# Where the cluster logits stand in PSUM, and where their comparison with the maximum is kept

## The chip, the cores and the metric

The program runs on one core of one Trainium2 chip. The metric is the device time of one execution in microseconds (us). Of the kernel before, three timed executions took 779.81, 781.78 and 782.66 us; their median, 781.78 us, is the time before. One further execution was recorded by the hardware profiler: it took 783.62 us, and the span from its first to its last recorded instruction is 781.8 us.

## The reference

Clustered attention is followed by a token-mixing layer. Every query and every key is given to one of 16 clusters, the one whose centroid it points at most; a query sees only the keys of its own cluster.

```python
q_assign = np.argmax(np.einsum('bhsd,hcd->bhsc', q_n, c_n), axis=-1)
k_assign = np.argmax(np.einsum('bhsd,hcd->bhsc', k_n, c_n), axis=-1)
mask = q_assign[:, :, :, None] == k_assign[:, :, None, :]
scores = scale * np.matmul(q, k.transpose(0, 1, 3, 2))
scores = np.where(mask, scores, -1000000000.0)
attn = softmax(scores)                  # written out there: minus the max, exp, over the sum + 1e-9
x = np.matmul(attn, v)                  # 4 batches x 8 heads x 768 tokens x 64
theta = x @ w_theta                     # x as 4 x 768 x 512 from here on
y = einsum(w_tok_r, x * cos(theta)) + einsum(w_tok_i, x * sin(theta))
u = x + y
out = u + np.maximum(u @ w_ch, 0.0)
```

The change touches only the `argmax`. It is computed as the first of the largest: the 16 logits of a token are compared with their maximum, the equal ones are weighed with the falling numbers 16, 15, ..., 1 (`wb`), and the largest weight names the cluster.

## The kernel before, in words

**Attention.** Two heads that lie in partitions 0 to 63 and 64 to 127 form a pair; there are 16 pairs (`pi`). A pair has 12 units `u`: two halves `a` of 384 queries, times six tiles `i` of 128 keys. For each unit and each head `j` of it TensorE computes a score tile `sc` of 128 keys x 384 queries in four matmuls (`score_products`: three products of high and low parts, and one that adds the mask and the row maximum), ScalarE takes the exponential out of PSUM (`exps`, L487), GpSimd adds the exponentials up (L498), and TensorE weighs the values with them (`weighted`, L559). Ten units ahead of the scores, TensorE computes the same products the other way round into tiles `m` (`max_products`), whose row maximum VectorE takes (`max_of`, L433).

**The order around the change is written out by hand.** The loop takes two units at a time, and each engine keeps the order in which the code issues. For the even unit `u` TensorE gets: the scores of `u` for both heads, interleaved (`both`); the scores of `u + 1` for head 0, interleaved with an `m` tile; the values of units `u - 2` and `u - 1` (eight `av` matmuls); then the pieces that are due at `u`; then the scores of `u + 1` for head 1, interleaved with another `m` tile. `score_products` and `max_products` are issued through `interleave` (L411). Preparatory work for later pairs is cut in pieces, due at units that stand in tables (`A_UNITS` for the clusters). `assign(pi)` loads a pair, computes its 16 x 2 logits per token (`lg`, copied to `lgs`), turns them so that tokens stand in the partitions (`turn_logits`, three 128 x 128 transposes into a tile `lt`, L300), takes the maximum and compares (`find_max`, L305 and L307), and in its next piece weighs and reduces (`first_of`, L312 and L314). The turn is due two units before the first scores of pair `pi - 1`, right after the eight `av` matmuls. Pairs 0 and 1 go through the same functions before the loop begins, so 14 pairs go through them in it.

**PSUM** has 8 banks. Pool `ps0` holds two tiles of two banks each for `m`; pool `ps` holds three single banks, which the score tiles use in turn, together with `lg`, `ot`, `mt` and `sm`; pool `ps_av` has one bank for `av`. A tile gets a bank when the earlier tile in it has been read for the last time: its first writer waits for that reader. An engine works off its own instructions strictly in order, so what stands behind a waiting matmul waits too.

**Then** the token-mixing layer follows: rotation angles (`tp`), mixing over tokens (`y`), and the channel layer (`cp`, `cy`). The change does not touch it.

Of the kernel before, what the change touches and what calls it, by code (L numbers as in the profile page):

```python
# [14 lines left out]
ALU = mybir.AluOpType  # L15
# [28 lines left out]
def kernel(  # L44
# [19 lines left out]
    nc = tc.nc  # L64
    B, H, D, S = qT.shape
    P = 128
    NP = H // 2
    NT = S // P
    C = cent.shape[0] // H
    DM = w_theta.shape[0]  # L70
    NCT = DM // P
    HS = S // 2
# [130 lines left out]
    def m_tile(name):  # L203
        return ps0.tile([P, 2, 512], F32, tag="m", name=name)

    def bank(name):
        return ps.tile([P, 512], F32, tag="bank", name=name)
# [58 lines left out]
    NG = HS // C  # L266

    wb = wc.unsqueeze(1).broadcast_to([P, NG, C])
# [23 lines left out]
        return lgs  # L292

    def turn_logits(pi, lgs):
        lt = (m_tile(f"lt{pi}")[:, 0] if pi > 1 else bank(f"lt{pi}"))[:, 0:HS]
        ltp = lt.rearrange("p (g a t c) -> p a g t c", a=2, t=NH, c=C)
        for t in range(HS // P):
            sl = slice(t * P, (t + 1) * P)

            nc.tensor.transpose(out=ltp[:, :, :, t], in_=lgs[:, sl], identity=identf)  # L300
        return lt.rearrange("p (g c) -> p g c", c=C)

    def find_max(pi, ltv):
        mx = pe.tile([P, NG], F32, tag="mxl", name=f"mxl{pi}")
        nc.vector.tensor_reduce(out=mx, in_=ltv, op=ALU.max, axis=AX.X)  # L305
        eq = pe.tile([P, NG, C], BF16, tag="eq", name=f"eq{pi}")
        nc.vector.tensor_tensor(  # L307
            out=eq, in0=ltv, in1=mx.unsqueeze(2).broadcast_to([P, NG, C]), op=ALU.is_equal)
        return eq

    def first_of(pi, eq):
        nc.vector.tensor_tensor(out=eq, in0=eq, in1=wb, op=ALU.mult)  # L312
        rr = pe.tile([P, NG], F32, tag="rr", name=f"rr{pi}")
        nc.vector.tensor_reduce(out=rr, in_=eq, op=ALU.max, axis=AX.X)  # L314
        return rr
# [9 lines left out]
    def turn_one_hot(pi, n):  # L325
        ot = bank(f"ot{pi}{n}").bitcast(BF16)[:, 0:S]
        for t in range(NT):
            nc.tensor.transpose(
                out=ot[:, t * P:(t + 1) * P], in_=ohp[:, n, t].rearrange("p j c -> p (j c)"), identity=identb)
        return ot  # L330

    def assign(pi):
# [7 lines left out]
        yield  # L340

        eq = find_max(pi, turn_logits(pi, lgs))
        yield

        rr = first_of(pi, eq)
        yield

# [392 lines left out]
    part_lo(0, "k", nc.gpsimd)  # L740
    keep_up(WAIT[2])
    ltv = turn_logits(0, lgs)
    load_v(0)
    g2 = assign(2)
    next(g2)
    rr = first_of(0, find_max(0, ltv))
    keep_up(WAIT[3])
    one_hot(rr)
# [16 lines left out]
    keep_up(NEXT)  # L765
    first_max(2, 0)
    ltv = turn_logits(1, lgs)
    first_max(2, 1)
    first_row()
    rr = first_of(1, find_max(1, ltv))  # L770
    one_hot(rr)
    first_max(3, 0)
# [23 lines left out]
    while u <= NUT or todo:  # L796
# [8 lines left out]
        if 0 <= u < NUT:  # L805
            both(score_products, u, exps)
            if u == 0:
# [4 lines left out]
                for n, x in ((1, "mk"), (0, "mq")):  # L812
                    nc.scalar.activation(
                        out=st[1][x], in_=turn_one_hot(1, n), func=AF.Identity,
# [32 lines left out]
    mx = mctx.enter_context(tc.tile_pool(name="mx", bufs=2))  # L847
# [264 lines left out]
```

## Time and profile before

| | |
|---|---|
| median of three timed executions | 781.78 us |
| the profiled execution, its own time | 783.62 us |
| its span | 781.8 us |
| PE busy | 772.4 us, 99% |
| VectorE (DVE) busy | 553.1 us, 71% |
| ScalarE (ACT) busy | 389.2 us, 50% |
| GpSimd (POOL) busy | 493.3 us, 63% |
| DVE busy from 100 to 400 us | 92.86, 92.91 and 91.79 us in each 100 us |
| granted TensorE clock | 0.998 |

Busy is the time in which an engine has an instruction under way. For PE that is not the same as useful work: matmuls are pipelined, and a matmul that starts late behind another one leaves no gap in the sum. Whether PE waits is read from the distance of the starts of its matmuls in the timeline. PEld is the loading of the stationary operand, which overlaps the matmul before it.

### The profile page before, as it was taken

Reading aid. Unit: us, or ns where it says so; the run is one execution under the profiler, and the core shown is the slowest. Engines: PE = TensorE matmul, PEld = TensorE weight load, DVE = VectorE, ACT = ScalarE, POOL = GpSimd, SP = SyncE. Lnnn points to the kernel's source line nnn. Section 1 sums busy time; section 2 is a strip of 40 time slices with the busy share of each in tenths; the row PEclk is TensorE's granted clock in tenths of the full one; section 3 lists DMA queues with packets and bytes.
Section 4 is the critical chain, followed back from the end, with each engine's and each line's share of the span. In section 5 each row is a group of like instructions: output and inputs, shape, how many; then the busy total and the mean of one; then the engine's idle time right before and its main releaser. Section 6 shows DMA issues by size and latency. Waiting matters only on the chain.

```text
span 781.8 us, 14392 instructions
## 1 busy us (share of the span) xinstructions
PE 772.4 (99%) x5580; PEld 571.6 (73%) x5580; DVE 553.1 (71%) x689; ACT 389.2 (50%) x781; POOL 493.3 (63%) x289
## 2 busy tenths in 40 slices
PE   8999999999999999999998999999999999999998
PEld 6666566656666665666664588898889988899998
DVE  7788999999899989999899577854344444533322
ACT  3566766676767666666655555432333132503310
POOL 4568888989999999988986575461225112422231
PEclk9999999999999999999999999999999999999999
DMA  4123323433343334333453476124101411120001
GB/s 143 42 60 100 113 77 113 137 109 97 120 140 107 102 115 144 124 108 129 131 201 115 104 198 193 28 56 147 27 14 28 162 28 28 17 92 15 1 21 62
DMA packets 82592, 73.23 MB, mean 94 GB/s; under 512 B 59538, under 2 KB 66844, under 8 KB 82140
## 3 DMA queue, kind: packets, MB, share of 16 engines
q1 hardware_dynamic: 82524, 72.32, 31.2%
q8 instruction: 44, 0.72, 0.4%
q14 instruction: 24, 0.20, 0.1%
HBM read 56.89 MB, written 15.31 MB: 92 GB/s over the span
## 4 chain that ended last, share of the span: by engine, by line
PE 87%; DVE 6%; DMA 3%; ACT 2%; issue 1%; SPq 1%; POOL 0%; DVEq 0%; ACTq 0%
PE sc L411 26%; PE y L980 20%; PE av L559 17%; PE tp L659 6%; PE cy L1003 5%; PE m L411 4%; PE cp L1003 3%; PE sm L526 2%; PE lg L287 2%; DMA wtmp<-in_w_ch_dram 1%; PE y L1003 1%; PE lt L300 1%; DVE nm L433 1%; PE mt L441 1%; PE idle L228 1%
## 5 line engine op out<-in xcount | busy, mean ns | idle before, releaser
L487 ACT ACTIVATE at<-sc 128x384 f32<-128x384 f32 x384 | 174.0, 493 | 96.3 <-PE sc L411 52.4
L433 DVE TENSOR_REDUCE nm<-m 128x1 f32<-128x768 f32 x192 | 180.2, 947 | 26.0 <-PE m L411 24.5
L498 POOL TENSOR_TENSOR acc<-at,at 128x768 f32<-128x768 f32 x64 | 126.0, 1969 | 37.5 <-ACT at L487 37.5
L411 PE MATMUL m<-hk,hq 64*128 64x384 f32 x384 | 147.4, 384 | 0.2 <-DVE nm L433 0.2
L559 PE MATMUL av<-at,vt 128*64 128x384 f32 x768 | 146.4, 502 | 0.2 <-ACT xt L574 0.2
L498 POOL TENSOR_TENSOR acc<-acc,at 128x768 f32<-128x768 f32 x64 | 132.5, 2070 | 10.0 <-ACT at L487 8.0
L931 POOL TENSOR_TENSOR zlc<-ab,zhc 128x512 fp32r<-128x512 f32 x24 | 32.4, 1351 | 158.5 <-ACT zhc L929 157.0
L411 PE MATMUL m<-mk,mq 64*128 64x384 f32 x384 | 128.2, 334 | 0.1
L411 PE MATMUL sc<-hq,hk 64*128 64x384 f32 x384 | 116.7, 390 | 1.1 <-ACT at L487 1.1
L411 PEld LDWEIGHTS sc<-hq,hk 64*128 64x128 f32 x384 | 55.1, 183 | 63.5 <-issue 25.3
L411 PE MATMUL sc<-hq,lk 64*128 64x384 f32 x384 | 97.1, 335 | 0.0
L411 PE MATMUL sc<-mq,mk 64*128 64x384 f32 x384 | 97.0, 335 | 0.0
L411 PE MATMUL sc<-lq,hk 64*128 64x384 f32 x384 | 96.7, 335 | 0.0
L559 PEld LDWEIGHTS av<-at,vt 128*64 128x64 f32 x768 | 46.8, 137 | 59.4 <-issue 54.1
L411 PEld LDWEIGHTS m<-hk,hq 64*128 64x128 f32 x384 | 70.4, 183 | 2.0 <-DVE nm L433 1.4
L411 PEld LDWEIGHTS m<-mk,mq 64*128 64x128 f32 x384 | 71.1, 185 | 0.8 <-DVE mk L376 0.4
L665 DVE TENSOR_SCALAR kk<-tp 128x512 int32<-128x512 f32 x24 | 16.4, 685 | 76.5 <-PE tp L659 76.5
L502 DVE TENSOR_TENSOR acc<-acc,acc 128x768 f32<-128x768 f32 x30 | 63.9, 2130 | 0.0
L632 ACT CAST xh<-xT 128x512 fp32r<-128x512 f32 x23 | 14.2, 619 | 95.8 <-PE tp L659 91.6
L994 POOL TENSOR_TENSOR ul<-xT,uh 128x384 fp32r<-128x384 f32 (+1 forms) x36 | 33.5, 959 | 35.5 <-ACT uh L993 33.8
L411 PEld LDWEIGHTS sc<-mq,mk 64*128 64x128 f32 x384 | 54.3, 185 | 0.0
L411 PEld LDWEIGHTS sc<-hq,lk 64*128 64x128 f32 x384 | 54.1, 185 | 0.0
(177 smaller groups left out, 1699.3 us busy)
## 6 DMA issues: line engine op xcount, KB each, us to landing
vt<-in_v_dram SPq DMA_DIRECT2D x16, 384.0 KB
rb<-sd SPq DMA_DIRECT2D x32, 192.0 KB
xT_d<-xt SPq DMA_DIRECT2D x16, 384.0 KB
xb<-xT_d SPq DMA_DIRECT2D x96, 64.0 KB
rawq<-in_qT_dram SPq DMA_DIRECT2D x15, 384.0 KB
rawk<-in_kT_dram SPq DMA_DIRECT2D x15, 384.0 KB
w<-in_wrT_dram SPq DMA_DIRECT2D x6, 768.0 KB
xT<-xT_d SPq DMA_DIRECT2D x3, 1536.0 KB
```

What stands on the lines that cost most here:

```text
L411: nc.tensor.matmul(out, lhsT=stat[r, cols], rhs=mov[r, over], start=start, stop=stop)
L433: nc.vector.tensor_reduce(out=s["nm", a][:, j, i // 2:i // 2 + 1], in_=s["m", j][:, :, 0:HS], op=ALU.max, axis=AX.XY, negate=True)
L487: last_exp[0] = nc.scalar.activation(out=s["at", a, i][:, j], in_=s["sc", j], func=AF.Exp, scale=SCALE)
L498: last_acc[0] = nc.gpsimd.tensor_tensor(out=s["acc", a, x], in0=prev, in1=at, op=ALU.add)
L502: nc.vector.tensor_tensor(out=s["acc", a, 0], in0=s["acc", a, 0], in1=s["acc", a, 1], op=ALU.add)
L559: nc.tensor.matmul(s["av"][64 * j:64 * j + 64], lhsT=s["vt"][:, i, j, :], rhs=s["at", a, i][:, j], start=(i == 0), stop=(i == NT - 1))
L659: nc.tensor.matmul(tp, lhsT=xx[:, c, :], rhs=w_th[c][k], start=(n == 0), stop=(n == 3 * NCT - 1))
L665: nc.vector.tensor_scalar_mul(kk, tp, INV_2PI)
L931: nc.gpsimd.tensor_tensor(out=zl, in0=tr, in1=zh.bitcast(F32), op=ALU.subtract)
L980: last_mix[0] = nc.tensor.matmul(y_at(b, d, c0, c1), lhsT=zz[:, d * P:(d + 1) * P], rhs=ww[:, c0:c1], start=first and lead, stop=last, ski ...
L994: nc.gpsimd.tensor_tensor(out=ul[:, d, :], in0=x, in1=uh[:, d, :].bitcast(F32), op=ALU.subtract)
L1003: nc.tensor.matmul(cp, lhsT=w_c[d][k][:, e * P:(e + 1) * P], rhs=uu[:, d, :], start=(n == 0), stop=(n == 3 * NCT - 1), skip_group_check=True)
```

## The change

Two things are changed, in three functions.

1. `turn_logits`: the turned logits `lt` of pairs 2 to 15 stand in a single bank of the scores' pool `ps` and no longer in a tile of the pool for `m`. Pairs 0 and 1 stood in a score bank already.
2. `find_max`: the comparison with the maximum (L306 now) is written back in place, as float32 in PSUM, and no longer as bf16 to SBUF. Its product with the weights (L309 now) reads it from PSUM, writes bf16 to SBUF, and is issued right behind the comparison; before, it was issued one piece later, in `first_of`, from SBUF to SBUF.

```diff
     def turn_logits(pi, lgs):
-        lt = (m_tile(f"lt{pi}")[:, 0] if pi > 1 else bank(f"lt{pi}"))[:, 0:HS]
+        lt = bank(f"lt{pi}")[:, 0:HS]
...
     def find_max(pi, ltv):
         mx = pe.tile([P, NG], F32, tag="mxl", name=f"mxl{pi}")
         nc.vector.tensor_reduce(out=mx, in_=ltv, op=ALU.max, axis=AX.X)
+        nc.vector.tensor_tensor(
+            out=ltv, in0=ltv, in1=mx.unsqueeze(2).broadcast_to([P, NG, C]), op=ALU.is_equal)
         eq = pe.tile([P, NG, C], BF16, tag="eq", name=f"eq{pi}")
-        nc.vector.tensor_tensor(
-            out=eq, in0=ltv, in1=mx.unsqueeze(2).broadcast_to([P, NG, C]), op=ALU.is_equal)
+        nc.vector.tensor_tensor(out=eq, in0=ltv, in1=wb, op=ALU.mult)
         return eq
 
     def first_of(pi, eq):
-        nc.vector.tensor_tensor(out=eq, in0=eq, in1=wb, op=ALU.mult)
         rr = pe.tile([P, NG], F32, tag="rr", name=f"rr{pi}")
```

No instruction is added or removed. On VectorE the product moves ahead of one row maximum of an `m` tile. In the rows below the first number in a name is the pair (`lt5`) or the unit (`sc35`, `m44`), the second the head; the last is a running number. This is VectorE's queue at the turn of pair 5, as a difference from before (-) to the change (+):

```order
 L305 TENSOR_REDUCE mxl5_1493<-lt5_1489 128x24
-L307 TENSOR_TENSOR eq5_1495<-lt5_1489,mxl5_1493 128x384
-L433 TENSOR_REDUCE nm42_1401<-m44_0_1498 128x1
-L312 TENSOR_TENSOR eq5_1495<-eq5_1495,wc_76 128x384
-L314 TENSOR_REDUCE rr5_1511<-eq5_1495 128x24
+L306 TENSOR_TENSOR lt5_1489<-lt5_1489,mxl5_1493 128x384
+L309 TENSOR_TENSOR eq5_1496<-lt5_1489,wc_76 128x384
+L433 TENSOR_REDUCE nm42_1401<-m44_0_1499 128x1
+L314 TENSOR_REDUCE rr5_1511<-eq5_1496 128x24
 L433 TENSOR_REDUCE nm42_1401<-m46_1_1528 128x1
```

The product stood behind the maximum of `m44_0`; it now stands ahead of it, and the reduction `rr` keeps its place.

On TensorE the order stays as it is, but what its matmuls wait for changes. The turn `lt5` stands eight rows ahead of these; the piece shown is the end of the scores of unit 35 for head 1, the scores of unit 36 for both heads, and the first two matmuls of unit 37. The name in brackets is the engine whose semaphore is waited for. Before:

```order
L411 MATMUL sc35_1_1497<-mq_2_158,mk_2_159 128x384
L411 MATMUL m44_0_1498<-mk_0_168,mq_0_167 128x384
L411 MATMUL sc36_0_1514<-hq_0_163,hk_0_165 128x384 [waits Activation_49]
L411 MATMUL sc36_1_1515<-hq_0_163,hk_0_165 128x384 [waits Activation_49]
L411 MATMUL sc36_0_1514<-lq_0_164,hk_0_165 128x384 [waits Pool_49]
L411 MATMUL sc36_1_1515<-lq_0_164,hk_0_165 128x384
L411 MATMUL sc36_0_1514<-hq_0_163,lk_0_166 128x384 [waits Pool_49]
L411 MATMUL sc36_1_1515<-hq_0_163,lk_0_166 128x384
L411 MATMUL sc36_0_1514<-mq_0_167,mk_0_168 128x384 [waits DMAHW4_49]
L411 MATMUL sc36_1_1515<-mq_0_167,mk_0_168 128x384 [waits DMAHW5_49]
L411 MATMUL sc37_0_1527<-hq_0_163,hk_0_165 128x384 [waits Activation_49]
L411 MATMUL m46_1_1528<-hk_0_165,hq_0_163 128x384 [waits DVE_49,PE_49]
```

And with the change:

```order
L411 MATMUL sc35_1_1498<-mq_2_158,mk_2_159 128x384
L411 MATMUL m44_0_1499<-mk_0_168,mq_0_167 128x384
L411 MATMUL sc36_0_1514<-hq_0_163,hk_0_165 128x384 [waits Activation_49]
L411 MATMUL sc36_1_1515<-hq_0_163,hk_0_165 128x384 [waits Activation_49]
L411 MATMUL sc36_0_1514<-lq_0_164,hk_0_165 128x384 [waits Pool_49]
L411 MATMUL sc36_1_1515<-lq_0_164,hk_0_165 128x384
L411 MATMUL sc36_0_1514<-hq_0_163,lk_0_166 128x384 [waits Pool_49]
L411 MATMUL sc36_1_1515<-hq_0_163,lk_0_166 128x384
L411 MATMUL sc36_0_1514<-mq_0_167,mk_0_168 128x384 [waits DMAHW4_49]
L411 MATMUL sc36_1_1515<-mq_0_167,mk_0_168 128x384 [waits DMAHW5_49]
L411 MATMUL sc37_0_1527<-hq_0_163,hk_0_165 128x384 [waits DVE_49,PE_49]
L411 MATMUL m46_1_1528<-hk_0_165,hq_0_163 128x384
```

The last two rows differ: `sc37_0` takes over the bank of `lt5` and waits for VectorE, and `m46_1` no longer follows `lt5` in a tile of `m`. Behind the same name in brackets two more waits differ, as the bank addresses and the semaphore counts of the two built programs say:

| first matmul of | before: bank, and who must have read it | with the change |
|---|---|---|
| `lt5` | a tile of `m`; VectorE's maximum of `m42_0` (L433) | score bank 5; ScalarE's exponential of `sc34_0` |
| `sc35_1` | score bank 4; exponential of `sc34_0` | bank 4; exponential of `sc34_1` |
| `sc36_0` | bank 5; exponential of `sc34_1` | bank 6; exponential of `sc35_0` |
| `sc36_1` | bank 6; exponential of `sc35_0` | bank 4; exponential of `sc35_1` |
| `sc37_0` | bank 4; exponential of `sc35_1` | bank 5; VectorE's product L309, the last reader of `lt5` |
| `m46_1` | the tile of `lt5`; VectorE's comparison L307 | a tile of `m` that has been free since before the turn |

The same holds, with other numbers, at each of the 14 pairs whose turn stands in the loop. GpSimd's and SyncE's queues are the same in both programs.

## The prediction

> **What bounds the kernel now.** I read the page first, for which engine the chain of work follows:
>
> ```profile
> PE 772.4 (99%) x5580; PEld 571.6 (73%) x5580; DVE 553.1 (71%) x689; ACT 389.2 (50%) x781; POOL 493.3 (63%) x289
> PE 87%; DVE 6%; DMA 3%; ACT 2%; issue 1%; SPq 1%; POOL 0%; DVEq 0%; ACTq 0%
> ```
>
> TensorE has something under way 99% of the time and carries 87% of the chain. So a change on VectorE is worth only what it moves on TensorE. A busy PE can still be a waiting PE, so the second view is the timeline of PE at one turn, that of pair 5:
>
> ```profile
> 100.61 0.49 PE L559 MATMUL av<-at,vt 128*64 128x384 f32 x2
> 101.04 0.55 PE L300 MATMUL lt<-identf,lgs 128*128 128x128 f32 x3
> 101.51 0.44 PE L411 MATMUL sc<-hq,hk 64*128 64x384 f32 x1
> 102.16 0.34 PE L411 MATMUL sc<-mq,mk 64*128 64x384 f32 x1
> 102.33 0.34 PE L411 MATMUL sc<-hq,hk 64*128 64x384 f32 x2
> 102.52 0.33 PE L411 MATMUL sc<-lq,hk 64*128 64x384 f32 x2
> 102.69 0.34 PE L411 MATMUL sc<-hq,lk 64*128 64x384 f32 x2
> 102.86 0.34 PE L411 MATMUL sc<-mq,mk 64*128 64x384 f32 x2
> 103.08 0.44 PE L411 MATMUL sc<-hq,hk 64*128 64x384 f32 x1
> 103.35 0.33 PE L411 MATMUL sc<-lq,hk 64*128 64x384 f32 x1
> 103.70 0.34 PE L411 MATMUL sc<-mq,mk 64*128 64x384 f32 x1
> 104.04 0.54 PE L559 MATMUL av<-at,vt 128*64 128x384 f32 x2
> ```
>
> The columns are start, duration, engine, line, operation. The starts matter. At 101.51 begins the score tile of unit 35 for head 1 (its last matmul starts at 102.16), at 102.33 the scores of unit 36 for both heads (the "x2": `sc36_0` and `sc36_1` side by side), at 103.08 `sc37_0`. Where nothing waits, a pair of matmuls starts 0.17 to 0.19 us after the last one (102.33, 102.52, 102.69, 102.86). Behind a wait it takes 0.27 us to the next (103.08 to 103.35). So PE works without a gap worth naming here, and every wait that is put into this row of matmuls lengthens it. ScalarE and VectorE at the same place:
>
> ```profile
> 98.85 1.40 ACT L487 ACTIVATE at<-sc 128x384 f32<-128x384 f32 x3 [0.22 <-PE sc L411]
> 102.53 0.49 ACT L487 ACTIVATE at<-sc 128x384 f32<-128x384 f32 x1 [2.28 <-PE m L411]
> 99.73 0.96 DVE L433 TENSOR_REDUCE nm<-m 128x1 f32<-128x768 f32 x1 [0.46 <-PE m L411]
> 101.62 0.56 DVE L305 TENSOR_REDUCE mxl<-lt 128x24 f32<-128x384 f32 x1 [0.93 <-PE lt L300]
> 102.22 0.56 DVE L307 TENSOR_TENSOR eq<-lt,mxl 128x384 bf16<-128x384 f32 x1
> 102.69 0.95 DVE L433 TENSOR_REDUCE nm<-m 128x1 f32<-128x768 f32 x1
> 103.55 1.66 DVE L312 TENSOR_TENSOR eq<-eq,wc 128x384 bf16<-128x384 bf16 x1
> 105.25 0.55 DVE L314 TENSOR_REDUCE rr<-eq 128x24 f32<-128x384 bf16 x1
> 105.72 0.95 DVE L433 TENSOR_REDUCE nm<-m 128x1 f32<-128x768 f32 x1
> ```
>
> The exponential at 102.53 is that of `sc35_1`; it ends at 102.53 + 0.49 = 103.02. The next view, the loads of PE, shows who held PE up at 103.08:
>
> ```profile
> 101.03 0.31 PEld L300 LDWEIGHTS lt<-identf,lgs 128*128 128x128 f32 x3 [0.60 <-DVE nm L433]
> 103.07 0.18 PEld L411 LDWEIGHTS sc<-hq,hk 64*128 64x128 f32 x1 [0.20 <-ACT at L487]
> 105.48 0.18 PEld L411 LDWEIGHTS sc<-hq,hk 64*128 64x128 f32 x1 [0.60 <-ACT w L142]
> ```
>
> `sc37_0` takes over the bank of `sc35_1` and starts 0.06 us after its exponential has ended. Today that costs almost nothing, because the four pairs of matmuls of unit 36 lie between the tile and the one that takes over its bank.
>
> **Part 1, the bank (the term that decides).** With `lt5` in a score bank, two banks are left for the scores around it. By the bank addresses `sc36_1` takes over the bank of `sc35_1`, whose last matmul starts at 102.16, one pair ahead of it. Before, it took over the bank of `sc35_0`, whose exponential had ended by 98.85 + 1.40 = 100.25. Nothing ahead of `sc35_1` moves: `lt5` waits for an exponential that ended by 100.25 and still starts at 101.04, when the `av` matmuls are through. So, from the rows above:
>
> - `sc36_0` makes its first matmul at 102.33; `sc36_1` has to wait for 103.02 and, as `sc37_0` does today, starts at 103.08. All of PE's queue stands behind it.
> - From there with the distances behind a wait: next pair at 103.08 + 0.27 = 103.35, then 103.52 and 103.70, and `sc37_0` at 103.87.
> - `sc37_0` needs its own bank, which VectorE must have left (part 2: about 103.42). It waits no more, and goes on at 0.17: 104.04, 104.22, 104.39 for its last three pairs. The `av` matmuls follow the last one by 104.04 - 103.70 = 0.34: at 104.73 and not at 104.04.
>
> That is **0.69 us later per turn**. Without the better distance behind `sc37_0` (0.27 instead of 0.17) it is 0.79; if `sc36_0` can run on in the gap, about 0.6. The number of turns in the loop comes from the answer for the tile: 48 transposes are 16 turns of three, and two of them stand ahead of the loop.
>
> ```profile
> L300 PE MATMUL lt<-identf,lgs x48: 272/273/330, 7.3 to 361.0; 128*128 128x128 f32 x48
> L307 DVE TENSOR_TENSOR eq<-lt,mxl x16: 557/558/558, 8.5 to 361.9; 128x384 bf16<-128x384 f32 x16
> L312 DVE TENSOR_TENSOR eq<-eq,wc x16: 357/1095/1672, 9.1 to 363.2; 128x384 bf16<-128x384 bf16 x16
> ```
>
> 14 x 0.69 = **+9.7 us** (bounds 14 x 0.6 = 8.4 and 14 x 0.79 = 11.1). Nothing on PE is idle enough to give it back: the exponentials, GpSimd's sums and VectorE's maxima follow PE's tiles and shift with them, and the transfers and the mixing layer start from the last scores.
>
> **Part 2, the comparison and the product.** L306 is not in the trace. Its nearest row is L307, the same reading of PSUM at 558 ns, never slowed by a neighbour (557 to 558 in 16); what writing to PSUM adds is not shown, so I bound it by nothing and by a second pass of the same length, 1.12 us. I take 0.56. L309 reads the same float32 tile from PSUM, so again 0.56, with 1.12 as the upper bound; it can hardly be under the 0.36 of L312's fastest. The sum: comparison from 102.22 to 102.78, product to 103.38 with gaps of 0.04 as between L305 and L307, and some 0.04 to the release: `sc37_0` may start at 103.42, against the 103.87 of part 1. So **0 on PE**. With one of the two at 1.12 the release is at 103.98: 0.1 per turn, 1.5 us. With both, 104.54: 0.67 per turn, 9.4 us. If part 1 cost nothing, `sc37_0` would still wait from 103.08 to 103.42.
>
> On VectorE the product falls from 19.3 us for 16 to 16 x 0.56 = 9.0 us: 10.3 us less work, but off the chain.
>
> ```profile
> L312 DVE TENSOR_TENSOR eq<-eq,wc 128x384 bf16<-128x384 bf16 x16 | 19.3, 1204 | 0.1
> L411 PEld LDWEIGHTS m<-mk,mq 64*128 64x128 f32 x384 | 71.1, 185 | 0.8 <-DVE mk L376 0.4
> PEld lt L300 <- DVE nm L433: 8.4, 14, 0.6
> ```
>
> What stands behind the product now is the maximum of `m44_0`: it would start at 103.42 and not at 102.69, and end at 104.37. The tile that waits for it is `m46_0`, which follows the `av` matmuls: today at 105.48 (the load above), so it is covered by over 1 us. `rr` becomes ready at about 104.9 and not at 105.8, so its readers wait less. In the second row, the mask `mk` (L376) once made PE wait 0.4 us, behind a slow product; I take that off: **-0.4**.
>
> The Trainium skill, "VectorE: DVE Perf Modes", section "The perf-mode tier table", speaks against this part: a `tensor_tensor` of bf16 in SBUF runs at double rate, and an operand in PSUM brings it down to single rate. The fastest L312 (357 ns) beside L307 (558 ns) agrees; the median of 1095 ns does not, since beside other work the bf16 product is the slow one here. By the rule alone VectorE would have 16 x 0.2 = 3.2 us more to do, and by the rows 10.3 us less; either is off the chain in the loop.
>
> Ahead of the loop, the product of pair 0 is on the chain, with no other work beside it; pair 1's is not, since the score tile that takes over its bank comes later:
>
> ```profile
> 9.11 0.36 DVE L312 TENSOR_TENSOR eq<-eq,wc 128x384 bf16<-128x384 bf16 x1
> 20.51 0.36 DVE L312 TENSOR_TENSOR eq<-eq,wc 128x384 bf16<-128x384 bf16 x1
> 21.45 0.44 PE L411 MATMUL sc<-hq,hk 64*128 64x384 f32 x2
> ```
>
> Pair 0 pays 0.56 - 0.36 = **+0.2**. Pair 1's bank would be free at 20.51 + 0.56 = 21.07, before 21.45: nothing.
>
> **The sum:** 9.7 - 0.4 + 0.2 = **+9.5 us**. The profiled execution took 783.62 us, with a span of 781.8; with the change they would be 793.1 and 791.3. The median of the three timed runs is 781.78, so I predict **791.3 us**.
>
> **Rivals.** *VectorE decides at `sc37_0`:* writing to and reading from PSUM in one bank doubles both new instructions, and the bank of `lt5` is free at 104.54 only. Then 9.7 + 9.4 - 0.4, and +1.3 for pair 0 (0.56 for the comparison, 0.76 for the product): +20, **802 us**. For it: no row shows VectorE writing to PSUM. Against: reading PSUM costs the same for every form shown.
>
> *The wait is hidden:* PE does not lose the 0.69 us, say because the end of a matmul is modelled and ScalarE really has `sc35_1` earlier, or because other short waits on ScalarE give the time back. Then -0.4 + 0.2, **781.6 us**. Against: the load at 103.07 shows PE starting right after that very exponential.
>
> *Faster, through the turn itself:* today `lt` waits for VectorE's maximum, 8.4 us over 14 turns in the waits' row above (0.60 each), and with the change it no longer does. If those were PE's time, and the pool for `m` were what holds it, the change would give -8.4 - 0.4 + 0.2 = -8.6: **773 us**. It decides only if PE could start the turn before 101.04. Against: the load at 105.48, where no turn stands, has the same 0.60 us in front of it, under the last `av` matmuls; so it is the pause of the loads at the end of any `av` group, and hidden. The maximum itself had ended at 99.73 + 0.96 = 100.69.
>
> **How the numbers follow.** My forecast gets 0.85, VectorE deciding 0.06, the hidden wait 0.05, the faster turn 0.04. The forecast's own range is 8.4 - 0.4 + 0.2 = +8.2 to 11.1 + 1.5 + 0.2 = +12.8, which with the 1.4 us by which the median of three may move gives 788.5 to 796. I widen it below by 0.5 us, for a price of the wait that other small waits soften: **788 to 796**. About 0.5% (3.9 us) is what a measurement of this kernel tells from no change. Slower by more than that: the forecast and VectorE deciding, 0.91; within it: 0.05; faster: 0.04.
>
> **What would show it.** In the changed kernel's timeline at a turn, a pair "x2" of first score matmuls falls apart: `sc36_0` starts 0.7 us ahead of `sc36_1`, whose load names ScalarE's exponential. The stretch from the turn's first transpose to the next `av` group grows from 3.0 to 3.7 us, and the distance of two turns by 0.7. L306 and L309 stand at about 0.56 each, without spread. VectorE's busy time falls by 10 us while the span grows. It is wrong if the x2 stays together at 102.33, if `sc37_0` waits for VectorE instead, or if the stretch of the loop outside the turns changes by more than 1 us.

## The result, and the profile after

The changed kernel takes 790.38 us (median of four, 789.55 to 792.1); the kernel before, with one more run beside it, 782.22 us. That is 8.2 us slower by the medians; the ratio on record, which is not that of the medians, is 1.0112 (95% interval 1.0081 to 1.0142). The profiled execution took 792.1 us with a span of 790.3 us, 8.5 us above the span before. The page of the changed kernel, busy times and the chain by engine:

```profile
PE 775.3 (98%) x5580; PEld 573.5 (73%) x5580; DVE 545.5 (69%) x689; ACT 388.0 (49%) x781; POOL 492.9 (62%) x289
PE 87%; DVE 6%; ACT 3%; DMA 2%; issue 1%; POOL 1%; SPq 0%; DVEq 0%; ACTq 0%; POOLq 0%
```

VectorE has 7.6 us less to do and the span is 8.5 us longer: the work that was saved was not on the chain. The place of the loss stands in PE's timeline at the turn of pair 5 (start, duration, engine, line, operation; in brackets the idle time before it and what ended it), then in the loads and in ScalarE's and VectorE's timelines there. Here and below, rows that the reading does not need, those of the `m` tiles above all, are left out:

```profile
102.81 0.55 PE L300 MATMUL lt<-identf,lgs 128*128 128x128 f32 x3
103.28 0.44 PE L411 MATMUL sc<-hq,hk 64*128 64x384 f32 x1
103.93 0.34 PE L411 MATMUL sc<-mq,mk 64*128 64x384 f32 x1
104.11 0.34 PE L411 MATMUL sc<-hq,hk 64*128 64x384 f32 x1
104.84 0.44 PE L411 MATMUL sc<-hq,hk 64*128 64x384 f32 x1 [0.40 <-ACT at L487]
104.85 0.61 PE L411 MATMUL sc<-lq,hk 64*128 64x384 f32 x2
105.12 0.51 PE L411 MATMUL sc<-hq,lk 64*128 64x384 f32 x2
105.47 0.34 PE L411 MATMUL sc<-hq,hk 64*128 64x384 f32 x1
106.43 0.87 PE L559 MATMUL av<-at,vt 128*64 128x384 f32 x4
...
104.84 0.18 PEld L411 LDWEIGHTS sc<-hq,hk 64*128 64x128 f32 x1 [0.72 <-ACT at L487]
211.17 0.18 PEld L411 LDWEIGHTS sc<-hq,hk 64*128 64x128 f32 x1 [0.72 <-ACT at L487]
...
104.30 0.49 ACT L487 ACTIVATE at<-sc 128x384 f32<-128x384 f32 x1 [2.28 <-PE m L411]
...
103.39 0.56 DVE L305 TENSOR_REDUCE mxl<-lt 128x24 f32<-128x384 f32 x1 [0.93 <-PE lt L300]
104.05 0.57 DVE L306 TENSOR_TENSOR lt<-lt,mxl 128x384 f32<-128x384 f32 x1
104.66 0.56 DVE L309 TENSOR_TENSOR eq<-lt,wc 128x384 bf16<-128x384 f32 x1
```

What stood in one row "x2" at 102.33 before is now two rows, `sc36_0` at 104.11 and `sc36_1` at 104.84. Its load waited 0.72 us, and names ScalarE's exponential, which ended at 104.30 + 0.49 = 104.79. The load at 211.17 is another turn, with the same 0.72. From the turn to the next `av` group it now takes 106.43 - 102.81 = 3.62 us, against 104.04 - 101.04 = 3.00 before. All 14 turns are alike in this: the traces have 3.60 to 3.64 us for each of them, and 2.99 to 3.00 before. The view of the tile gives the first and the last transpose of all turns and the prices of the two new instructions:

```profile
L300 PE MATMUL lt<-identf,lgs x48: 272/273/330, 7.5 to 368.9; 128*128 128x128 f32 x48
L306 DVE TENSOR_TENSOR lt<-lt,mxl x16: 567/567/567, 8.7 to 369.8; 128x384 f32<-128x384 f32 x16
L309 DVE TENSOR_TENSOR eq<-lt,wc x16: 557/557/558, 9.3 to 370.4; 128x384 bf16<-128x384 f32 x16
```

From the first turn to the last it is 361.4 us; before, by the row in the prediction, 361.0 - 7.3 = 353.7. That is 7.7 us, with the last turn's 0.62 behind it 8.3 of the 8.5 us. The other 0.2 lies ahead of the first turn, which starts at 7.5 us and not at 7.3, before anything that was changed has run. The rest of the program, the mixing layer included, only starts later: from the start of the last turn to the end it takes 421.7 us, against 421.1 before, and the 0.6 between them is that turn's own.

### The profile page after: what moved, and what is told of

Read it like the earlier page. It is cut to its first block, busy times and chain, and to the rows that moved or that the text cites. A ratio compares the mean times of both kernels' runs of the same rounds, so it can differ in the third digit from the quotient of the medians.

```text
span 790.3 us, 14406 instructions
## 1 busy us (share of the span) xinstructions
PE 775.3 (98%) x5580; PEld 573.5 (73%) x5580; DVE 545.5 (69%) x689; ACT 388.0 (49%) x781; POOL 492.9 (62%) x289
## 4 chain that ended last, share of the span: by engine, by line
PE 87%; DVE 6%; ACT 3%; DMA 2%; issue 1%; POOL 1%; SPq 0%; DVEq 0%; ACTq 0%; POOLq 0%
PE sc L411 25%; PE y L980 19%; PE av L559 17%; PE tp L659 6%; PE m L411 5%; PE cy L1003 5%; PE cp L1003 3%; PE sm L526 2%; PE lg L287 1%; DMA wtmp<-in_w_ch_dram 1%; PE y L1003 1%; ACT at L487 1%; PE lt L300 1%; PE mt L441 1%; DVE nm L433 1%
## 5 line engine op out<-in xcount | busy, mean ns | idle before, releaser
L433 DVE TENSOR_REDUCE nm<-m 128x1 f32<-128x768 f32 x192 | 181.0, 948 | 40.1 <-PE m L411 21.2
L498 POOL TENSOR_TENSOR acc<-at,at 128x768 f32<-128x768 f32 x64 | 126.0, 1968 | 46.4 <-ACT at L487 46.4
L498 POOL TENSOR_TENSOR acc<-acc,at 128x768 f32<-128x768 f32 x64 | 132.4, 2069 | 9.5 <-ACT at L487 7.6
L411 PE MATMUL sc<-hq,hk 64*128 64x384 f32 x384 | 121.7, 391 | 6.6 <-ACT at L487 6.5
L411 PEld LDWEIGHTS sc<-hq,hk 64*128 64x128 f32 x384 | 57.8, 184 | 71.0 <-ACT at L487 25.6
L411 PE MATMUL sc<-lq,hk 64*128 64x384 f32 x384 | 100.6, 339 | 0.0
L411 PE MATMUL sc<-hq,lk 64*128 64x384 f32 x384 | 99.6, 336 | 0.0
L411 PE MATMUL sc<-mq,mk 64*128 64x384 f32 x384 | 99.5, 336 | 0.0
L502 DVE TENSOR_TENSOR acc<-acc,acc 128x768 f32<-128x768 f32 x30 | 65.0, 2167 | 0.0
L411 PEld LDWEIGHTS sc<-mq,mk 64*128 64x128 f32 x384 | 56.8, 186 | 0.0
L411 PEld LDWEIGHTS sc<-hq,lk 64*128 64x128 f32 x384 | 56.6, 186 | 0.0
L411 PEld LDWEIGHTS sc<-lq,hk 64*128 64x128 f32 x384 | 55.8, 187 | 0.0
```

Source lines behind the costliest of these rows:

```text
L411: nc.tensor.matmul(out, lhsT=stat[r, cols], rhs=mov[r, over], start=start, stop=stop)
L433: nc.vector.tensor_reduce(out=s["nm", a][:, j, i // 2:i // 2 + 1], in_=s["m", j][:, :, 0:HS], op=ALU.max, axis=AX.XY, negate=True)
L498: last_acc[0] = nc.gpsimd.tensor_tensor(out=s["acc", a, x], in0=prev, in1=at, op=ALU.add)
L502: nc.vector.tensor_tensor(out=s["acc", a, 0], in0=s["acc", a, 0], in1=s["acc", a, 1], op=ALU.add)
```

## The experiments

Times are compared with the runs of the kernel before that were made beside them; their median is 782.1 us for the first four kernels, 782.62 for the next three, 783.18 for the last two.

### Only the bank

```diff
 # the kernel before, with:
-        lt = (m_tile(f"lt{pi}")[:, 0] if pi > 1 else bank(f"lt{pi}"))[:, 0:HS]
+        lt = bank(f"lt{pi}")[:, 0:HS]
```

> Only the bank is changed: the turned logits stand in a score bank; the comparison goes to SBUF and the product follows one piece later, as in the kernel before. The banks are then taken over in another order: sc36_1 takes the bank of lt5 itself (last read by the comparison L307) and sc37_0 that of sc35_1. Theory (what costs is the one score tile that follows too closely behind the tile whose bank it takes): the comparison would end 1.27 us after the first score matmul of unit 35, head 1 (101.51 to 102.78 in the trace of before), so sc36_1 waits 0.5 us and not 0.73; with 0.63 from its start to sc37_0, as in the changed kernel, a turn costs 0.37 us more than before, 14 turns 5.2 us: about 787. Rival A (only the bank matters, whoever reads it): as the changed kernel, about 8 us over before, 790. Rival B (the new comparison and product cost the time, the bank nothing): 782.

786.58 us, ratio 1.0058 (1.004 to 1.0077): 4.5 us slower, near the 787 of the theory, and clear of 790 and of 782. That it is so near is in part luck: by the rows below a turn costs 105.92 - 102.48 = 3.44 us against 3.00, so 0.44 more and not the 0.37 of the theory; the last section tells where the profiled execution makes up for it. PE's loads and matmuls and VectorE at the turn of pair 5 in this kernel:

```profile
104.33 0.18 PEld L411 LDWEIGHTS sc<-hq,hk 64*128 64x128 f32 x1 [0.54 <-PE m L411]
...
102.48 0.55 PE L300 MATMUL lt<-identf,lgs 128*128 128x128 f32 x3
...
104.36 0.41 PE L411 MATMUL sc<-hq,hk 64*128 64x384 f32 x1 [0.24 <-DVE eq L307]
...
105.92 1.51 PE L559 MATMUL av<-at,vt 128*64 128x384 f32 x8
...
103.66 0.56 DVE L307 TENSOR_TENSOR eq<-lt,mxl 128x384 bf16<-128x384 f32 x1
```

`sc36_1` waits in this kernel too, 0.54 us instead of 0.72, but for another reader: the comparison, which ends at 104.22. So the bank alone is enough to make the kernel slower, but through another wait than in the changed kernel: the 4.5 us are no part of the 8.2. How much a turn costs follows from which bank the tile behind gets and when its last reader ends. That is a wait, not a price of the bank as such.

### Only the comparison and the product

```diff
 # the changed kernel, with:
-        lt = bank(f"lt{pi}")[:, 0:HS]
+        lt = (m_tile(f"lt{pi}")[:, 0] if pi > 1 else bank(f"lt{pi}"))[:, 0:HS]
```

> Only the comparison and the product are changed; the turned logits stay in a tile of m for pairs 2 to 15. Theory: no score tile waits at the turn, but m46_1, which follows lt5 in its tile, now waits for the product and not for the comparison: it starts 0.24 us later (103.42 instead of 103.18 on the clock of before), 14 x 0.24 = 3.4 us, less 0.4 for the mask of pair 3, more 0.2 ahead of the loop: +3.2, about 785. Rival A (the two VectorE instructions are off the chain and nothing waits for them): 782. Rival B (they are what costs): 790.

785.1 us, ratio 1.0038 (1.0026 to 1.0049): 3.0 us slower, where the theory said 3.2. Here too the total is nearer than the working: in the trace each of the 14 turns takes 3.34 or 3.35 us from its start to the next `av` group, 0.35 more than before and not the 0.24 of the theory. The load of `m46_1` and the product that it waits for:

```profile
103.97 0.18 PEld L411 LDWEIGHTS sc<-hq,hk 64*128 64x128 f32 x1 [0.19 <-ACT at L487]
104.38 0.18 PEld L411 LDWEIGHTS m<-hk,hq 64*128 64x128 f32 x1 [0.23 <-PE sc L411]
...
103.71 0.56 DVE L309 TENSOR_TENSOR eq<-lt,wc 128x384 bf16<-128x384 f32 x1
```

The product ends at 104.27, and `m46_1` starts 0.41 us behind `sc37_0`, where it was 0.07 behind the 103.07 of the kernel before, in whose loads it stands so:

```profile
103.14 0.18 PEld L411 LDWEIGHTS m<-hk,hq 64*128 64x128 f32 x1
```

The label in brackets of the row at 104.38 names PE's own last matmul; that it is the product that was waited for, I take from its end at 104.27 and from `m46_1` following in the bank of `lt`. Neither half of the change is free, then: the bank alone makes `sc36_1` wait for a reader, and the product alone makes `m46_1`, the next tile in the bank that `lt` keeps longer.

### The turn ahead of the `av` matmuls, with its control

```diff
 # the changed kernel, and as the control the kernel before, each with:
-    A_UNITS = (-9, -4, -2, -1, 2, 2, 3, 6, 7, 7.9)
+    A_UNITS = (-9, -4, -2.5, -1, 2, 2, 3, 6, 7, 7.9)
-    A_THIRD = (4, 5, 6, 6, 7.5, 9, 11, 12)
+    A_THIRD = (3.5, 5, 6, 6, 7.5, 9, 11, 12)
```

> The changed kernel with the turn due half a unit earlier, so that its three transposes stand ahead of the eight av matmuls of 1.44 us and not behind them. The same score bank, the same VectorE instructions. In the built program sc36_1 then follows lt5 in its bank and waits for the product L309. Theory: VectorE takes the maximum of m44_1 first (to 100.69 on the clock of before), then the three steps to 102.5; sc36_1 would have started at 102.42, so the wait is 0.1 us or less, and a turn costs nothing to 0.1 us: 0 to 1.4 us in all, less 0.4 and more 0.2, so 781.5 to 783.5. Rival (two banks for the scores around a turn are too few wherever it stands): 788 to 791.

> The control for the run before: the kernel before, with the turn due half a unit earlier, in the tile of m. Theory: the place of the turn alone is worth little: the short wait at m46_1 (0.07 us a turn) goes, 14 x 0.07 = 1 us: 781 to 782. Rival (the place alone moves PE by several us): outside 779 to 785.

Both missed. The changed kernel came to 787.17 us (1.0061, 1.004 to 1.0081), between the theory's 783.5 and the rival's 788; the control to 784.92 us (1.0035, 1.0016 to 1.0053), so the place alone costs 2.8 us. I had worked out VectorE's times at pair 5 alone. In the control, the turn of pair 5 waits 0.25 us, which is the pause behind any group of scores (in the kernel before it stands in front of the `av` groups); that of pair 9 waits 0.75, and all from pair 8 on wait 0.71 to 0.75:

```profile
99.54 0.31 PEld L300 LDWEIGHTS lt<-identf,lgs 128*128 128x128 f32 x3 [0.25 <-DVE sq L544]
204.28 0.31 PEld L300 LDWEIGHTS lt<-identf,lgs 128*128 128x128 f32 x3 [0.75 <-DVE nm L433]
...
96.67 1.54 DVE L502 TENSOR_TENSOR acc<-acc,acc 128x768 f32<-128x768 f32 x1
200.89 2.46 DVE L502 TENSOR_TENSOR acc<-acc,acc 128x768 f32<-128x768 f32 x1
203.28 0.94 DVE L433 TENSOR_REDUCE nm<-m 128x1 f32<-128x768 f32 x1
```

The sum of exponentials in front (L502) takes 2.46 us there and not 1.54, so the maximum whose tile the turn needs ends at 204.22 only. With the turn in a score bank the same lateness comes out one step further on, at the product, which by my expectation left no wait to the tile behind it:

```profile
206.81 0.56 DVE L309 TENSOR_TENSOR eq<-lt,wc 128x384 bf16<-128x384 f32 x1
207.01 0.34 PE L411 MATMUL sc<-hq,hk 64*128 64x384 f32 x1
207.51 0.41 PE L411 MATMUL sc<-hq,hk 64*128 64x384 f32 x1 [0.16 <-DVE eq L309]
```

The product ends at 206.81 + 0.56 = 207.37, and the matmul that waited for it, of `sc36_1`'s counterpart, starts at 207.51, 0.5 us behind its neighbour at 207.01. So moving the turn did take the wait of 0.72 us for ScalarE away, and put a shorter one for VectorE in its place. The rival, a general want of banks, is settled by the starts of the turns. From the turn of pair 4 to that of pair 8 there are 177.95 - 73.74 us here, 26.05 a turn; the kernel before has 25.98 and the changed kernel 26.60. With the same two banks left for the scores a turn costs 0.07 us there, near the 0.1 of the theory; from pair 8 on, where the product is late, a turn takes 26.32. So it is not the number of banks that costs.

### The product behind the maximum, from PSUM

```diff
 # the changed kernel, with the product in its old place:
     def find_max(pi, ltv):
...
-        nc.vector.tensor_tensor(out=eq, in0=ltv, in1=wb, op=ALU.mult)
-        return eq
+        return eq, ltv
     def first_of(pi, eq):
+        eq, ltv = eq
+        nc.vector.tensor_tensor(out=eq, in0=ltv, in1=wb, op=ALU.mult)
```

> The changed kernel with the product put back into its later piece, behind the maximum of m44_0, but still reading the comparison from PSUM. The banks are taken over as in the changed kernel: sc36_1 waits for the exponential of sc35_1, sc37_0 for the product. Theory (VectorE has only some 0.2 us to spare there: in the changed kernel the product ends at 105.22 and sc37_0 starts at 105.47): with the maximum of 0.95 us in front of it the product ends near 106.0, sc37_0 waits 0.5 to 0.6 us more, 14 turns 7 to 8.4 us: 797 to 799. Rival (only the exponential holds PE, VectorE has time enough): 790, as the changed kernel.

798.01 us, ratio 1.0205 (1.0179 to 1.0231), as the theory said. The loads at the turn of pair 5, and the product, L313 in this kernel:

```profile
106.99 0.18 PEld L412 LDWEIGHTS sc<-hq,hk 64*128 64x128 f32 x1 [0.72 <-ACT at L488]
108.20 0.18 PEld L412 LDWEIGHTS sc<-hq,hk 64*128 64x128 f32 x1 [0.57 <-PE sc L412]
...
107.54 0.55 DVE L313 TENSOR_TENSOR eq<-lt,wc 128x384 bf16<-128x384 f32 x1
```

The first wait is that of the changed kernel, untouched; a second one of 0.57 us has come behind it, at `sc37_0`, and ends 0.1 us after the product (107.54 + 0.55 = 108.09). The product itself ends 0.7 us later in its turn than in the changed kernel (the turn starts at 104.95, so 3.14 us behind its start; there it is 105.22 - 102.81 = 2.41). So in the changed kernel VectorE is the next to decide, with little to spare, and the product's earlier place is what keeps it from deciding.

### A shorter hold of the bank, with its control

```diff
 # the changed kernel, and as the control the kernel before, each with:
     def exps(u, j):
...
-        last_exp[0] = nc.scalar.activation(out=s["at", a, i][:, j], in_=s["sc", j], func=AF.Exp, scale=SCALE)
+        at, n = s["at", a, i], (32 if j == 1 and u % NU == NU - 1 else HS)
+        last_exp[0] = nc.scalar.activation(out=at[:, j, 0:n], in_=s["sc", j][:, 0:n], func=AF.Exp, scale=SCALE)
+        if n < HS:
+            last_exp[0] = nc.scalar.activation(out=at[:, j, n:HS], in_=at[:, 0, n:HS], func=AF.Exp, scale=SCALE)
```

> The changed kernel, with the exponential that the waiting tile waits for cut in two: at each pair's last unit (13 of the 14 turns), head 1, 32 of the 384 columns are read from the score tile, and an instruction behind it fills the other 352 from the exponentials of head 0 in SBUF. That part of the result is left out; the bank is given free after the first, short instruction. ScalarE has more to do, not less. Theory (PE waits for just this reader): the first instruction takes about 0.2 us and not 0.49, sc36_1 starts 0.27 us earlier, 13 turns 3.5 us: 786 to 788. Rival (the time is lost elsewhere, to fewer banks or to VectorE): 790 or, with one more instruction of 0.47 us on ScalarE, above.

> The control: the same cut of the exponential in the kernel before, the same part of the result left out. There sc37_0 takes over that bank, behind four pairs of matmuls, and waits about 0.05 us. Theory: 0 to 0.1 us a turn to gain, 0 to 1.3 us: 781 to 782.5. Rival (a shorter hold of the bank is worth the same everywhere): 778 to 779.

788.13 us for the changed kernel (1.0073, 1.0052 to 1.0094), just above the 786 to 788 of the theory; 780.48 us for the control (0.9977, 0.9966 to 0.9988), below the 781 that it gave. Over their own runs of the kernel before, the changed kernel gains 2.7 us (8.2 to 5.5) and the control 2.1, so the totals do not tell the two apart. Nor does the gain by turn: 0.26 us in the changed kernel (3.62 to 3.36), where the theory had 0.27, but 0.21 in the control (3.00 to 2.79), where it had 0.1 at most. What differs is the wait that goes. The wait of `sc36_1` and the short exponential in the changed kernel, and in the control the place where the load of `sc37_0` used to wait:

```profile
103.74 0.20 ACT L488 ACTIVATE at<-sc 128x32 f32<-128x32 f32 x1 [2.27 <-PE m L411]
103.98 0.18 PEld L411 LDWEIGHTS sc<-hq,hk 64*128 64x128 f32 x1 [0.42 <-ACT at L488]
...
102.86 0.34 PE L411 MATMUL sc<-mq,mk 64*128 64x384 f32 x2
103.04 0.33 PE L411 MATMUL sc<-hq,hk 64*128 64x384 f32 x1
103.21 0.33 PE L411 MATMUL sc<-lq,hk 64*128 64x384 f32 x1
103.82 1.51 PE L562 MATMUL av<-at,vt 128*64 128x384 f32 x8
```

With the exponential 0.29 us shorter, `sc36_1` waits 0.30 us less: it is this reader that it waits for. In the control no wait is left: the second matmul of `sc37_0` follows the first after 0.17 us and not 0.27, and the `av` group stands at 103.82 and not at 104.04. A wait of 0.05 us had cost a turn 0.2 us in the kernel before.

### The other half of the array first

The last two runs asked whether what such a short wait costs beyond itself can be avoided, in both kernels. In pairs of a score tile and an `m` tile, the `m` tile's matmul now goes first.

```diff
 # the kernel before and the changed kernel, each with:
-        interleave(score_products(u, j), max_products(v, 1 - j))
+        pair = [score_products(u, j), max_products(v, 1 - j)]
+        interleave(*(pair if j else pair[::-1]))
```

> The kernel before, where the m tile's matmul goes first in the pairs of the scores of u + 1 for head 0 (order m, sc, m, sc and not sc, m, sc, m). In the traces the first matmul of that score tile waits 0.05 us for an exponential in every second unit, some 80 times in all, and the pair behind it then comes after 0.27 us and not after 0.17: about 0.15 us lost each time, and with the shorter exponential a turn became 0.22 us shorter. Theory (what is dear is the restart of both halves of the array, so a wait of 0.05 us in one of them alone costs 0.05): 0.1 us less at about 65 places outside the turns: 6 us less, about 776. Rival (the queue is in order and the restart costs the same whichever matmul waits): 782.

> The same reordering in the changed kernel. At the turns sc36_1 still waits for the exponential of sc35_1 and nothing is gained there; sc37_0 waits no more for an exponential. Theory: the same 6 us less outside the turns, about 784, so that the distance of the two kernels stays at 8 us. Rival: 790.

781.91 us for the kernel before with this order (0.998, 0.9963 to 0.9996), 790.58 us for the changed one (1.0095, 1.0065 to 1.0125). The theory's 6 us are not there; both kernels came out as the rival had it, 782 and 790. The timeline of PE in the first of the two, away from a turn:

```profile
107.09 0.33 PE L411 MATMUL m<-hk,hq 64*128 64x384 f32 x1
107.14 0.44 PE L411 MATMUL sc<-hq,hk 64*128 64x384 f32 x1
107.26 0.33 PE L411 MATMUL m<-mk,mq 64*128 64x384 f32 x1
107.41 0.33 PE L411 MATMUL sc<-lq,hk 64*128 64x384 f32 x1
```

The `m` tile's half does run on at 0.17 us, as meant, but the score half takes its 0.27 after the wait all the same, and the `av` matmuls wait for the later half. The distance of the two kernels stayed at 8.7 us, as both theories had it. No version here beats the kernel before by as much as 0.5%.

## Why the prediction was right

**The step that decided** was part 1, the bank that `sc36_1` takes over: predicted 0.69 us for each of 14 turns, measured 0.62 at pair 5 and 0.60 to 0.65 at the others. The predicted start of `sc36_1`, 0.75 us behind `sc36_0`, is 0.73 in the trace. What was a little too large was the way from there to `sc37_0`: 0.79 predicted, 0.63 measured, because `sc36_0` goes on at once (104.84 and 104.85) and does not have to start again; the lower bound of 0.6 was given for just that. The gain at `sc37_0` that I had counted (0.10 for the better distance) was eaten on the way, since its partner `m46_1` came 0.18 us behind it and not 0.10 (105.65 against 103.18 before), and the `av` matmuls follow the later of the two. 14 x 0.62 = 8.7 us in place of 9.7.

**Part 2.** The comparison written to PSUM costs 567 ns and the product 557 ns, against 0.56 taken for each, without spread. The upper bounds were far off. The product ends at 105.22 where `sc37_0` starts at 105.47, so VectorE does not decide. But the 0.25 us between them are less than the prediction had (0.45 from the release to `sc37_0`), and the late product shows that the margin is small. Of the 10.3 us that VectorE was to save on the product, its busy time shows 7.6 us net (553.1 to 545.5). The sums of exponentials (L502) take 1.1 of the other 2.7: 65.0 us and not 63.9; where the rest went was not followed. On PE the saving is worth 0, as predicted. The Trainium skill, "GPSIMD Engine Reference", section "1. Specifications", says that GpSimd shares its SBUF interfaces with VectorE, with contention for instructions that have two SBUF inputs. The traces agree: L312, with two of them, ran 357 and 358 ns at pairs 0 and 1, where GpSimd was idle, and over 1 us at each of the 13 turns where it met GpSimd's sum L498 from pair 3 on; at pair 5 it starts at 103.55 beside this row of the kernel before and ends at 105.21:

```profile
103.17 1.83 POOL L498 TENSOR_TENSOR acc<-acc,at 128x768 f32<-128x768 f32 x1 [0.21 <-ACT at L487]
```

L309, with one input in PSUM, ran 557 to 558 ns everywhere.

**The small terms.** The wait for the mask of pair 3 is gone (-0.4). In its row in the groups of the changed kernel, only the masks ahead of the loop are left, and so it is in the kernel with only the bank changed (second row):

```profile
L411 PEld LDWEIGHTS m<-mk,mq 64*128 64x128 f32 x384 | 71.1, 185 | 0.4 <-ACT mq L754 0.3 <-DVE mk L731 0.2
...
L411 PEld LDWEIGHTS m<-mk,mq 64*128 64x128 f32 x384 | 71.0, 185 | 0.4 <-ACT mq L754 0.3
```

So the size of the term was right, but its reason is not shown. The prediction put the wait down to the slow product ahead of the mask. With only the bank changed the product is as slow as before (1.67 us at pair 3), and the wait is gone all the same, since PE comes 0.44 us later behind that turn.

The product of pair 0 takes 0.20 us more ahead of the loop (+0.2). So 8.7 - 0.4 + 0.2 = 8.5 us. The spans differ by just that, but 0.2 of it lies ahead of the first turn, so from there on the sum is 0.2 too large. The medians differ by 8.2, and 791.3 was predicted for 790.38.

**The rivals.** *VectorE decides* fell with the price of L306; the late product shows what it would have been like, at 798 us for a product 0.7 us later. *The wait is hidden* fell with the 0.72 us in the loads. Its price in the prediction was wrong by the prediction's own part 2: if part 1 had cost nothing, `sc37_0` would still have waited from 103.08 to 103.42, 14 x 0.34 = 4.8 us, and the rival stood for about 786 and not for 781.6. With the product alone, in the other pool, a tile behind did wait for it, and a turn cost 0.35 us. *Faster, through the turn itself* fell as argued: the load of `lt` now waits for no maximum and still shows the 0.60 us in front of it.

```profile
102.80 0.31 PEld L300 LDWEIGHTS lt<-identf,lgs 128*128 128x128 f32 x3 [0.60 <-issue]
PEld lt L300 <- issue: 8.0, 14, 0.6
```

The same pause, 8.0 us over 14 turns, has merely lost its name.

## What to carry to other kernels

Before a tile is given to another pool, follow who takes over its place and whose last reader that tile then waits for: the price lies with the tiles behind it in the ring, and a ring of three that lends out one can make a neighbour follow too closely. Where the loan stands in the order matters: half a unit earlier the same loan cost 0.07 us at the early turns. A busy share of 99% tells nothing of such a wait; the starts of the matmuls and the loads' releasers do. And a time worked out at one turn of a loop holds for that turn: look at a late one too, where the helpers may run behind.

## What was not expected

A wait of 0.05 us cost PE about 0.2 us a turn in the kernel before (3.00 against 2.79 us without it). The traces show one part of the difference: the next matmul of the tile that waited follows after 0.27 us instead of 0.17, whether its first matmul is issued ahead of that of the `m` tile or behind it.

In six of the eleven profiled executions, those of the kernel before and of the changed one among them, the weights' preparation holds a pause of 1.5 to 1.7 us on VectorE: one instruction (L153) takes 2.05 to 2.22 us, in the other five 0.56. It collides with GpSimd's sum of exponentials (L498), which starts at nearly the same time. Here are the two in the kernel before, then in the one with only the bank changed:

```profile
415.83 1.82 POOL L498 TENSOR_TENSOR acc<-at,at 128x768 f32<-128x768 f32 x1 [1.97 <-ACT at L487]
415.85 2.22 DVE L153 SCALAR_TENSOR_TENSOR spare<-spare,spare 128x384 int32<-128x384 int32 x1
...
422.06 2.22 POOL L498 TENSOR_TENSOR acc<-at,at 128x768 f32<-128x768 f32 x1 [2.00 <-ACT at L487]
422.05 0.56 DVE L153 SCALAR_TENSOR_TENSOR spare<-spare,spare 128x384 int32<-128x384 int32 x1
```

In each of the eleven one of the two is slow and the other is not. Where VectorE's is slow, GpSimd's sum has started 0.01 to 0.23 us ahead of it and takes 1.81 to 1.87 us, and VectorE's ends 0.4 us behind it; where VectorE's takes 0.56 us, the two start within 0.01 us of each other and the sum takes 2.22 to 2.24. So little decides which it is that it may change from one execution to the next, but no kernel here has two traces to show it.

The pause is one reason why a total says less than a turn. With only the bank changed, 14 turns cost 14 x 0.44 = 6.2 us more, but the span is only 4.5 us longer (786.3 against 781.8). It starts its first turn 0.5 us later (7.8 against 7.3), takes 5.3 us more from the start of the first turn to that of the last (13 x 0.44, less the 0.4 of the mask of pair 3), and from the start of the last turn to the end, where the pause stands, 1.3 us less (419.8 against 421.1). The kernel with only the comparison and the product changed, which has no pause either, is even 2.8 us shorter in that last stretch (418.3): its span is only 1.5 us longer (783.3 against 781.8), though its turns cost 14 x 0.35 = 4.9 us. Which part of these 1.3 and 2.8 us is the pause was not followed, and the timed runs, from which the 4.5 and 3.0 us of the two kernels come, have no trace to tell whether they had it.
